# Layer two's rows scaled and split in 768-column operations, weights prepared at 0.64 steps, one branch hinted

## The chip, the cores and the metric

One core of a Trainium2 chip runs the whole program. The metric is the device time of one execution in microseconds (us). The engines are TensorE (PE in the rows; PEld is its weight load), VectorE (DVE), ScalarE (ACT), GpSimd (POOL) and SyncE (SP, which here only issues transfers). TensorE's clock has two levels, 1.2 and 2.4 GHz; the rows give the granted share of the higher one.

## The reference

Three stages in a row, all in fp32, on 7168 tokens of 192 columns.

```python
# 1. dynamic convolution: 8 heads of 24 columns, 7 taps, weights by softmax
out[b, s, h] = sum_k softmax(weight_gen)[b, s, h, k] * x_pad[b, s + k, h]
# 2. mixture of experts 1: 8 experts, two per token
noisy = x @ w_gate + log1p(exp(x @ w_noise)) * noise
top2, top2_w = two largest of noisy, softmax over the two
out[t] = sum over the two e:  top2_w * (relu(x[t] @ w1[e]) @ w2[e])     # w1 192x1024, w2 1024x192
# 3. mixture of experts 2: 8 experts, one per token
logits = normalised(x) @ normalised(expert_emb).T / tau
e = argmax(logits);  gate = softmax(logits)[e]
out[t] = gate * (relu(x[t] @ w1[e]) @ w2[e])
```

## The kernel before

**Layout.** Token columns: the 7168 tokens are 56 columns of 128. Work on tokens goes in chunks of four columns (`CH`), that is tiles of 128 partitions x 4 x 192 = 768 elements. Each layer handles its tokens in three groups of columns, 0 to 24, 24 to 40 and 40 to 56. Once a group is scored, its tokens are ranked by expert on the chip and listed into tiles of 256 tokens of one expert. GpSimd gathers a tile's rows from a DRAM table `T` (L1031), and scatters its results into `YB` (layer one, two rows per token) or the output (layer two) (L1115).

**Precision.** A row is scaled by a power of two (`pow2`, L254 to L256) and split into a high and a low fp16 part; products are made of three or five fp16 products that sum in PSUM. Weights are scaled and split in the same way: `prep_gen` reads fp32 weights, squares and sums them, scales them (L357, ScalarE), subtracts (L359, VectorE) and stores the fp16 parts to a DRAM table `WS`, from which SyncE loads a tile's weights (L1049).

**The tile loop.** Layer one has 64 tiles, 0 to 63, layer two 36, 64 to 99. Tiles 51 to 54 and the last four are rarely needed; they lie in a branch (`rare`, L1337), entered on a flag. Each iteration interleaves the first product of the next tile (`first_product`, L1081, ReLU copy L1083, its low part L1084) with the second product of this one (`second_product`, L1107). After a group of products each calls `bgq.point(share)`.

**Background queue.** Everything else is emitted by generators. A point adds its share (0.845) to two credits, one for VectorE (the real part) and one for ScalarE (the imaginary part); a generator goes on while both are above zero, and each `yield` takes what the step is said to cost. A `yield "lag"` ends a generator's turn at this point. There are eight points in an iteration with a full tile. A third thread holds `prep_rest`, layer two's weight preparation: it ignores the credits and makes `P_STEPS` steps per point once both attention groups 0 and 1 are emitted. `combine_gen(g)` loads the two result rows of a chunk from `YB` (`combine_load`, four buffers, two per chunk), scales one by its gate (L1162) and adds the other (L1169); it may start once the loop has reached tile 55 for groups 0 and 1, or 64 for group 2, and only when layer two's weights are `ready`. `post_chunk` then takes norms (L452), scales and splits the chunk, transposes it on TensorE (L492) and makes the scores (L506, L509). `ctl` picks experts (`choose2`, whose first operation is L529), ranks them and lists the tiles; its end allows a group's first gather. Two iterations ahead of a group's first gather, `bgq.finish` emits whatever is left of that group.

**What sets the order.** The program is planned before it runs: on each engine, within the stretch between two branches, the planner takes what it holds to be ready, by priority, which is the place of emission. Layer two's preparation has a low priority of its own (`R_LOW`), except for its loads, stores and small products, which take the place where they are emitted (`urgent`). Products of the background queue are held behind the tile product that was last emitted (`after_product`). Across the branch nothing moves.

**The branch.** `tc.If(flag > 0, preferred_fallthrough_block=False)` asks for the code of the side that is not entered right behind the comparison. Every engine loads the flag into a register and compares; the side not entered also settles the semaphores that the skipped block would have raised (L1337 in the rows).

Of the kernel before, what the change touches and what calls it, by code (L numbers as in the profile page):

```python
# [7 lines left out]
F32 = mybir.dt.float32  # L8
# [15 lines left out]
CH = 4  # L24
# [3 lines left out]
R_CTL, R_ATT, R_PREP, R_B, R_BODY = 0, 2000, 2000, 18000, 20000  # L28
C_AT = 5
R_LOW = 40000  # L30
P_STEPS = 0.54
SHARE = 0.845
ORDER = (0, 0, 1, 0, 1, 0, 1, 1)
LA = 3
# [44 lines left out]
def two_moe(ctx: ExitStack, tc: tile.TileContext, x, wgen, w_gate, w_noise, noise, w1a, w2a, emb, tau, w1b, w2b, out):  # L79
# [361 lines left out]
    isx = consts.tile([128, 2, NCOL], F32, name="isx")  # L441
    y_loads = []

    def post_chunk(l, acc, a, lg, g0, rows_i, done):
        ne = 16 if l == 0 else 8
        s = slice(a, a + CH)
        if rows_i is None:
# [5 lines left out]
        yield 1.6j  # L453
        pow2(nrm[:, l, s].bitcast(I32), sx[:, l, s], isx[:, l, s], CH, 194, 60)
        yield 0.4
        if l == 0:
            xs = att.tile([128, CH, D], F32, name="xs", bufs=1)
            for c in range(CH):
                A.activation(xs[:, c], acc[c], AF.Copy, scale=sx[:, l, a + c:a + c + 1])
            yield 1.4j  # L460
            A.activation(rows[:, :, 0:192], xs, AF.Copy)
            yield 0.7j
            for o, h, n in ((256, 0, 128), (192, 128, 64)):
                V.tensor_tensor(rows[:, :, o:o + n], xs[:, :, h:h + n], rows[:, :, h:h + n], op=ALU.subtract)
            V.tensor_copy(rows_i[:, :, 192:196].bitcast(F32), isx[:, 0, s, None].to_broadcast([128, CH, 4]))
            state["accs"] -= 1
            yield 1.0
        else:
            for c in range(CH):
                A.activation(rows[:, c, 0:192], acc[c], AF.Copy, scale=sx[:, l, a + c:a + c + 1])  # L470
            yield 1.4j
            for c in range(CH):
                for o, h, n in ((256, 0, 128), (192, 128, 64)):
                    V.scalar_tensor_tensor(rows[:, c, o:o + n], acc[c][:, h:h + n], sx[:, l, a + c:a + c + 1], rows[:, c, h:h + n],  # L474
                                           op0=ALU.mult, op1=ALU.subtract)
            state["accs"] -= 1
            yield 1.3
        if l == 0:
            write_rows(0, rows_i, a, CH)
        yield from lag(3)  # L480
# [670 lines left out]
    def combine_gen(g):  # L1151
        a, b = L2.groups[g]
        while 1 not in ready:
            yield None
        nxt = combine_load(a)
        yield from lag(5)
        for c0 in range(a, b, CH):
            y = nxt
            if c0 + CH < b:
                nxt = combine_load(c0 + CH)  # L1160
            for c in range(CH):
                V.tensor_scalar(y[0][:, c], y[0][:, c], gates[:, 0, c0 + c:c0 + c + 1], None, op0=ALU.mult)  # L1162
            yield 0.6
            while state["accs"] >= 2:
                yield None
            state["accs"] += 1
            acc = att.tile([128, CH, D], F32, name="acc")
            for c in range(CH):
                V.scalar_tensor_tensor(acc[:, c], y[1][:, c], gates[:, 1, c0 + c:c0 + c + 1], y[0][:, c], op0=ALU.mult, op1=ALU.add)  # L1169
            yield 1.1  # L1170
            bgq.chain(post_chunk(1, [acc[:, c] for c in range(CH)], c0, lgs[1][g], a, rows2[g][:, c0 - a:c0 - a + CH], dones[1][g]))

    def att_gen(g):
        a, b = L1.groups[g]
# [158 lines left out]
    def rare(block):  # L1333

        l, L = tiles[block[0]][0:2]
        c = L.np + KEEP
        with tc.If(nc.values_load(flag_i[l][0:1, c:c + 1], min_val=0, max_val=1) > 0, preferred_fallthrough_block=False):  # L1337
            new_block()
            state["rare"] = True
            for i in block:  # L1340
# [23 lines left out]
    for j, i in enumerate(seq):  # L1364
        later = seq[j + 1:j + 4]
        if len(later) >= LA:
            if later[LA - 1] in need:
                bgq.finish(need[later[LA - 1]])
            gather(later[LA - 1])
        one = first_product(later[0], bgq.point) if later else iter(())  # L1370
        two = second_product(i, bgq.point)
        for part in ORDER:
# [47 lines left out]
```

## Time and profile before

| | |
|---|---|
| time, median of three runs (lowest, highest) | 1059.68 us (1053.8, 1062.92) |
| time of the profiled execution | 1060.5 us |
| its span, first to last instruction | 1058.7 us |
| mean granted TensorE clock | 0.931 |
| TensorE products busy | 917.6 us, 87% of the span |
| TensorE weight loads busy | 826.0 us, 78% |
| VectorE busy | 691.1 us, 65% |
| ScalarE busy | 584.3 us, 55% |
| GpSimd busy | 380.9 us, 36% |
| DMA, over the span | 236.32 MB moved, mean 223 GB/s |

The profile is one execution on the chip. "Busy" is the time in which an engine had an instruction running; register work, branches, semaphores and the issue of transfers do not count as busy. A group of instructions is named by its line in the kernel, its engine and operation, and `out<-in` by the program's names; a bracket or a last field such as `5.89 <-issue` is the time that the engine stood idle ahead of it and what ended that; `issue` means that the profile shows nothing it waited for. `xh` as an output of L452, L470 and L474 is layer two's table of split rows, which lies in the same memory as the input.

### The profile page before, as it was taken

To read this page: it belongs to the slowest core of one execution; us is meant where nothing else is said; L and a number is where in the kernel's file an instruction comes from. 1 tells how busy PE (TensorE), PEld (TensorE's weight loads), DVE (VectorE), ACT (ScalarE), POOL (GpSimd) and SP (SyncE) were. 2 spreads that over 40 slices of the span, in tenths; PEclk is the share of its full clock that TensorE was granted. 3 is DMA by queue.
4 is the path that set the end of the run, shared out by engine and by line. 5 is a ranking of instruction groups with operands and counts; after the bars stand their busy time and mean duration, and the time that the engine had idled before them with its cause. 6 is when DMAs were issued, how large, how long until landed. Compare 5 with 4: busy or idle time off the path is not lost.

```text
span 1058.7 us, 26447 instructions
## 1 busy us (share of the span) xinstructions
PE 917.6 (87%) x9714; PEld 826.0 (78%) x9714; DVE 691.1 (65%) x1935; ACT 584.3 (55%) x1289; POOL 380.9 (36%) x368
## 2 busy tenths in 40 slices
PE   5993149998989999999998998995698999999996
PEld 2551139887979989989998987884587899999996
DVE  8996969898969879735353436679866753333331
ACT  2989426665548685445464546587156444444442
POOL 1000044434343653344444342321444344444522
PEclk9995559999989999999999998997698999999999
DMA  8789773745387756557989876852874734867661
GB/s 273 213 269 286 246 264 102 222 167 184 125 256 246 227 166 235 198 187 247 341 315 365 296 248 202 280 162 89 269 237 174 281 113 161 289 219 275 240 214 45
DMA packets 96392, 236.32 MB, mean 223 GB/s; under 512 B 13439, under 2 KB 64223, under 8 KB 87808
## 3 DMA queue, kind: packets, MB, share of 16 engines
q1 hardware_dynamic: 79360, 200.35, 55.3%
q0 software_dynamic: 16896, 34.20, 10.6%
q8 instruction: 80, 1.31, 0.5%
q14 instruction: 56, 0.46, 0.1%
HBM read 230.60 MB, written 57.90 MB: 273 GB/s over the span
## 4 chain that ended last, share of the span: by engine, by line
PE 53%; DVE 18%; DMA 11%; ACT 7%; issue 7%; POOL 2%; SPq 2%; POOLq 0%; DVEq 0%; ACTq 0%
PE ph L1081 24%; PE py L1107 21%; DMA xg<-t,gx 3%; DMA wb<-ws 3%; DVE tmp L407 2%; PE pt L1059 2%; DVE hl L1084 2%; DMA tmp<-yb 2%; PE py L434 2%; DVE acc L422 2%; ACT wo L357 1%; DVE wt L1084 1%; DVE acc L1169 1%; DVE xh L474 1%; DMA xh<-in_moe_w_dram 1%
## 5 line engine op out<-in xcount | busy, mean ns | idle before, releaser
L1081 PE MATMUL ph<-xt,wb 128*128 128x256 f16 x3360 | 429.1, 280 | 21.0 <-DMA wb<-ws 7.6
L1081 PEld LDWEIGHTS <-wb 128*128 128x128 f16 x3360 | 332.2, 100 | 64.2 <-issue 17.1
L1107 PE MATMUL py<-wb,hh 128*128 128x192 f16 x2688 | 357.5, 247 | 3.8 <-issue 3.8
L1083 ACT ACTIVATE hh<-ph 128x512 f16<-128x512 f32 (+1 forms) x368 | 210.0, 577 | 261.2 <-PE ph L1081 202.7
L1031 POOL DMA_INDIRECT xg<-t,gx x176 | 177.9, 1011 | 340.9 <-DVE gx L837 135.6
L1107 PEld LDWEIGHTS <-hh 128*128 128x128 f16 x2816 | 254.0, 98 | 9.7 <-issue 5.7
L1115 POOL DMA_INDIRECT yb<-ys,sx x116 | 126.3, 1089 | 202.6 <-ACT ys L1112 178.4
L1084 DVE SCALAR_TENSOR_TENSOR hl<-ph,hh 128x512 f16<-128x512 f32 (+1 forms) x184 | 117.3, 641 | 116.0 <-ACT hh L1083 83.1
L1084 DVE SCALAR_TENSOR_TENSOR wt<-ph,hh 128x512 f16<-128x512 f32 x184 | 125.6, 686 | 99.5 <-ACT hh L1083 78.1
L1107 PE MATMUL py<-wb,wt 128*128 128x192 f16 x736 | 182.0, 247 | 0.0
L1107 PE MATMUL py<-wb,hl 128*128 128x192 f16 x608 | 150.2, 247 | 0.0
L1112 ACT ACTIVATE ys<-py,sc 128x192 f32<-128x192 f32 x176 | 64.7, 416 | 89.8 <-PE py L1107 73.4
L1115 POOL DMA_INDIRECT out_dram<-ys,sx x60 | 61.8, 1029 | 102.0 <-ACT ys L1112 88.5
L407 DVE TENSOR_TENSOR tmp<-xh,wt 128x768 f32<-128x768 f32 x90 | 84.5, 949 | 0.3 <-PE ph L434 0.2
L1061 ACT ACTIVATE xt<-pt 128x768 f16<-128x768 f16 x84 | 67.7, 807 | 11.6 <-PE pt L1059 6.0
L1107 PEld LDWEIGHTS <-wt 128*128 128x128 f16 x736 | 72.5, 98 | 0.9 <-issue 0.7
L1092 DVE TENSOR_SCALAR sc<-xg,csl 128x2 f32<-128x2 f32 (+1 forms) x92 | 21.0, 228 | 75.4 <-ACT ys L1112 64.9
L1107 PEld LDWEIGHTS <-hl 128*128 128x128 f16 x672 | 66.0, 98 | 0.2
L1059 PE MATMUL pt<-identh,xg 128*128 128x128 f16 x528 | 47.0, 222 | 18.9 <-DMA xg<-t,gx 14.7
L1059 PEld LDWEIGHTS <-xg 128*128 128x128 f16 x528 | 36.9, 99 | 21.9 <-DMA xg<-t,gx 17.6
L359 DVE SCALAR_TENSOR_TENSOR wo<-xh,wsc,wo 128x384 f16<-128x384 f32 (+1 forms) x70 | 44.8, 667 | 2.8 <-ACT wo L357 1.9
L498 ACT ACTIVATE xt<-rb 128x768 f16<-128x768 f16 x56 | 42.7, 808 | 6.7 <-PE rb L492 6.5
(304 smaller groups left out, 992.7 us busy)
## 6 DMA issues: line engine op xcount, KB each, us to landing
wb<-ws SPq DMA_DIRECT2D x84, 1024.0 KB
wb<-ws SPq DMA_DIRECT2D x84, 768.0 KB
ws<-wo SPq DMA_DIRECT2D x16, 768.0 KB
tmp<-yb SPq DMA_DIRECT2D x28, 384.0 KB
ws<-wo SPq DMA_DIRECT2D x16, 512.0 KB
ws<-wo SPq DMA_DIRECT2D x32, 256.0 KB
xh<-ws SPq DMA_DIRECT2D x8, 1024.0 KB
xh<-in_moe_w_dram SPq DMA_DIRECT2D x10, 768.0 KB
```

Of the source, the lines that this page charges most:

```text
L359: V.scalar_tensor_tensor(lo, v, sc[:, c:c + 1], h, op0=ALU.mult, op1=ALU.subtract)
L407: V.tensor_mul(dst.rearrange("p t (h g) -> p (t h) g", g=G), xv, w)
L498: A.activation(xt.rearrange("p a n -> p (a n)"), pa[:, 0:768], AF.Copy)
L1031: PL.indirect_dma_start(out=xg[:, h], out_offset=None, in_=T[l][0:rows_in], in_offset=bass.IndirectOffsetOnAxis(ap=gidx[l][:, u + h:u + h ...
L1059: PE.transpose(pt[:, j, h], xg[:, h, 128 * b:128 * b + 128], identh)
L1061: A.activation(xt.rearrange("p j h n -> p (j h n)"), pt.rearrange("p j h n -> p (j h n)"), AF.Copy)
L1081: state["pe"] = mark = PE.matmul(ph[:, q, :n], s, m, start=j == 0, stop=j == 4)
L1083: A.activation(hh[:, fs, :n], ph[:, :, :n], AF.Relu)
L1084: state["pin"] = V.scalar_tensor_tensor(hl[:, fs, :n], ph[:, :, :n], 0.0, hh[:, fs, :n], op0=ALU.max, op1=ALU.subtract)
L1107: state["pe"] = PE.matmul(py[:, h], t[:, f, hs], w2[:, f, c], start=f == 0 and j == 0, stop=f == 7 and j == 2)
L1112: A.activation(ys[:, h], py[:, h], AF.Copy, scale=sc[:, h:h + 1])
L1115: d = PL.indirect_dma_start(out=dst, out_offset=bass.IndirectOffsetOnAxis(ap=sidx[l][:, u + h:u + h + 1], axis=0), in_=ys[:, h], in_offset ...
```

## The change

Four edits.

- `P_STEPS`, the steps of layer two's weight preparation per point, goes from 0.54 to 0.64.
- The gate scaling in `combine_gen`, four VectorE operations of 192 columns, becomes one of 768 columns with the gate broadcast. The credits asked go from 0.6 and 1.1 to 0.9 and 1.6.
- `post_chunk` for layer two scales the chunk with one VectorE operation of 768 columns into a single fp32 buffer `xs`, converts it with one ScalarE copy of 768 columns, and subtracts with two VectorE operations of 512 and 256 columns. Before, ScalarE made four scaled copies and VectorE eight scale-and-subtract operations. The credits asked go from 1.4j and 1.3 to 0.9, 0.7j and 1.1. Layer one's operations stay, but it asks 1.1 in place of 1.0 at the end. The chunk's buffer is counted as free once it is scaled.
- The branch gets a label and no preferred side, and ahead of the products of the iteration that ends at layer one's rare block a hint "LikelyTaken" for that label is given to TensorE, behind the last product emitted. Layer two's branch, behind the last tile, gets no hint.

```diff
@@ -28,7 +28,7 @@
 R_CTL, R_ATT, R_PREP, R_B, R_BODY = 0, 2000, 2000, 18000, 20000
 C_AT = 5
 R_LOW = 40000
-P_STEPS = 0.54
+P_STEPS = 0.64
 SHARE = 0.845
 ORDER = (0, 0, 1, 0, 1, 0, 1, 1)
 LA = 3
@@ -441,7 +441,7 @@
     isx = consts.tile([128, 2, NCOL], F32, name="isx")
     y_loads = []
 
-    def post_chunk(l, acc, a, lg, g0, rows_i, done):
+    def post_chunk(l, acc, a, lg, g0, rows_i, done, whole=None):
         ne = 16 if l == 0 else 8
         s = slice(a, a + CH)
         if rows_i is None:
@@ -453,28 +453,22 @@
         yield 1.6j
         pow2(nrm[:, l, s].bitcast(I32), sx[:, l, s], isx[:, l, s], CH, 194, 60)
         yield 0.4
+        xs = att.tile([128, CH, D], F32, name="xs", bufs=1)
         if l == 0:
-            xs = att.tile([128, CH, D], F32, name="xs", bufs=1)
             for c in range(CH):
                 A.activation(xs[:, c], acc[c], AF.Copy, scale=sx[:, l, a + c:a + c + 1])
             yield 1.4j
-            A.activation(rows[:, :, 0:192], xs, AF.Copy)
-            yield 0.7j
-            for o, h, n in ((256, 0, 128), (192, 128, 64)):
-                V.tensor_tensor(rows[:, :, o:o + n], xs[:, :, h:h + n], rows[:, :, h:h + n], op=ALU.subtract)
+        else:
+            V.tensor_tensor(xs, whole, sx[:, l, s, None].to_broadcast([128, CH, D]), op=ALU.mult)
+            yield 0.9
+        state["accs"] -= 1
+        A.activation(rows[:, :, 0:192], xs, AF.Copy)
+        yield 0.7j
+        for o, h, n in ((256, 0, 128), (192, 128, 64)):
+            V.tensor_tensor(rows[:, :, o:o + n], xs[:, :, h:h + n], rows[:, :, h:h + n], op=ALU.subtract)
+        if l == 0:
             V.tensor_copy(rows_i[:, :, 192:196].bitcast(F32), isx[:, 0, s, None].to_broadcast([128, CH, 4]))
-            state["accs"] -= 1
-            yield 1.0
-        else:
-            for c in range(CH):
-                A.activation(rows[:, c, 0:192], acc[c], AF.Copy, scale=sx[:, l, a + c:a + c + 1])
-            yield 1.4j
-            for c in range(CH):
-                for o, h, n in ((256, 0, 128), (192, 128, 64)):
-                    V.scalar_tensor_tensor(rows[:, c, o:o + n], acc[c][:, h:h + n], sx[:, l, a + c:a + c + 1], rows[:, c, h:h + n],
-                                           op0=ALU.mult, op1=ALU.subtract)
-            state["accs"] -= 1
-            yield 1.3
+        yield 1.1
         if l == 0:
             write_rows(0, rows_i, a, CH)
         yield from lag(3)
@@ -1158,17 +1152,16 @@
             y = nxt
             if c0 + CH < b:
                 nxt = combine_load(c0 + CH)
-            for c in range(CH):
-                V.tensor_scalar(y[0][:, c], y[0][:, c], gates[:, 0, c0 + c:c0 + c + 1], None, op0=ALU.mult)
-            yield 0.6
+            V.tensor_tensor(y[0], y[0], gates[:, 0, c0:c0 + CH, None].to_broadcast([128, CH, D]), op=ALU.mult)
+            yield 0.9
             while state["accs"] >= 2:
                 yield None
             state["accs"] += 1
             acc = att.tile([128, CH, D], F32, name="acc")
             for c in range(CH):
                 V.scalar_tensor_tensor(acc[:, c], y[1][:, c], gates[:, 1, c0 + c:c0 + c + 1], y[0][:, c], op0=ALU.mult, op1=ALU.add)
-            yield 1.1
-            bgq.chain(post_chunk(1, [acc[:, c] for c in range(CH)], c0, lgs[1][g], a, rows2[g][:, c0 - a:c0 - a + CH], dones[1][g]))
+            yield 1.6
+            bgq.chain(post_chunk(1, [acc[:, c] for c in range(CH)], c0, lgs[1][g], a, rows2[g][:, c0 - a:c0 - a + CH], dones[1][g], acc))
 
     def att_gen(g):
         a, b = L1.groups[g]
@@ -1334,7 +1327,7 @@
 
         l, L = tiles[block[0]][0:2]
         c = L.np + KEEP
-        with tc.If(nc.values_load(flag_i[l][0:1, c:c + 1], min_val=0, max_val=1) > 0, preferred_fallthrough_block=False):
+        with tc.If(nc.values_load(flag_i[l][0:1, c:c + 1], min_val=0, max_val=1) > 0, label=f"rare{l}"):
             new_block()
             state["rare"] = True
             for i in block:
@@ -1367,6 +1360,10 @@
             if later[LA - 1] in need:
                 bgq.finish(need[later[LA - 1]])
             gather(later[LA - 1])
+        if later and later[0] > i + 1:
+
+            with after_product():
+                tc.mark_branch_hint_location(f"rare{tiles[i][0]}", "LikelyTaken", [mybir.EngineType.PE])
         one = first_product(later[0], bgq.point) if later else iter(())
         two = second_product(i, bgq.point)
         for part in ORDER:
```

## Rows read from the trace of the kernel before

**Rows 1.** The page: busy tenths and granted TensorE clock in 40 equal slices of the span.

```profile
PE   5993149998989999999998998995698999999996
...
PEclk9995559999989999999999998997698999999999
```

**Rows 2.** The chain that ended last: start us, length us, what.

```profile
475.08 1.98 PE py L1107 x24
...
483.75 1.98 PE py L1107 x24
...
642.69 4.19 DMA tmp<-yb
...
679.80 8.16 DMA tmp<-yb
...
759.77 4.42 PE ph L1081 x20
```

**Rows 3.** Windows: length, each engine's busy us (instructions), granted clock, DMA share, GB/s.

```profile
633.00:642.50 9.50, 3.93 (x22) 2.83 (x23) 0.92 (x2) 1.05 (x3) 2.02 (x2) 0.64 0.56 205
642.50:672.00 29.50, 27.26 (x290) 25.04 (x288) 26.30 (x90) 22.92 (x66) 11.30 (x11) 1.00 0.73 236
672.00:695.00 23.00, 23.00 (x256) 21.87 (x254) 12.63 (x35) 12.57 (x30) 5.35 (x6) 1.00 0.82 281
695.00:759.00 64.00, 42.45 (x543) 35.06 (x542) 54.94 (x281) 39.27 (x110) 19.86 (x14) 0.78 0.48 151
759.00:1059.00 300.00, 280.13 (x3104) 262.17 (x3103) 135.24 (x397) 131.78 (x279) 119.56 (x117) 0.97 0.60 206
230.00:430.00 200.00, 188.60 (x2079) 176.00 (x2077) 172.64 (x487) 126.80 (x269) 87.64 (x80) 0.97 0.62 204
```

**Rows 4.** One line each, windows behind 632 us: duration min/median/max ns, first and last start.

```profile
L492 PE MATMUL rb<-identh,xh x168: 216/219/314, 695.4 to 820.6; 128*128 128x128 f16 x168
...
L529 DVE TENSOR_REDUCE mx<-lg x3: 277/286/334, 724.2 to 826.6; 128x16 f32<-128x128 f32 x2, 128x24 f32<-128x192 f32 x1
...
L1031 POOL DMA_INDIRECT xg<-t,gx x16: 952/957/1002, 751.4 to 788.2; - x16
...
L359 DVE SCALAR_TENSOR_TENSOR wo<-xh,wsc,wo x8: 599/604/607, 648.1 to 670.9; 128x384 f16<-128x384 f32 x8
```

**Rows 5.** The branch's line: duration min/median/max ns, first and last start us.

```profile
L1337 PEldq COMPARE_BRANCH  x4: 81/1954/5529, 631.7 to 1049.9; - x4
...
L1337 POOLq INC_SWDGE_SEM  x2: 852/1542/2231, 640.3 to 1054.0; - x2
```

**Rows 6.** Timeline of TensorE from 632 to 650 us: start, length, products, idle before.

```profile
638.57 4.04 PE L1081 MATMUL ph<-xt,wb 128*128 128x256 f16 x20 [5.89 <-issue]
...
648.96 1.26 PE L1081 MATMUL ph<-xt,wb 128*128 128x256 f16 x10
```

**Rows 7.** Timeline of VectorE around chunks of layer two: start, length, operations, idle before.

```profile
646.91 1.23 DVE L1162 TENSOR_SCALAR tmp<-tmp,gates 128x192 f32<-128x192 f32 x4 [2.89 <-DMA tmp<-yb]
...
785.44 1.00 DVE L1162 TENSOR_SCALAR tmp<-tmp,gates 128x192 f32<-128x192 f32 x4
...
791.93 1.92 DVE L474 SCALAR_TENSOR_TENSOR xh<-acc,sx,xh 128x128 f16<-128x128 f32 x8
```

**Rows 8.** All groups by line and shape: busy us, mean ns of one.

```profile
L1083 ACT ACTIVATE hh<-ph 128x512 f16<-128x512 f32 x336 | 197.7, 595 | 243.1 <-PE ph L1081 201.3 <-issue 14.1 <-PE pt L1059 9.3
...
L407 DVE TENSOR_TENSOR tmp<-xh,wt 128x768 f32<-128x768 f32 x90 | 84.5, 949 | 0.3 <-PE ph L434 0.2
...
L470 ACT ACTIVATE xh<-acc,sx 128x192 f16<-128x192 f32 x56 | 21.0, 446 | 5.3 <-DVE isx L256 3.7 <-DVE wo L359 1.6
...
L461 ACT ACTIVATE rows<-xs 128x768 f16<-128x768 f32 x14 | 11.8, 846 | 0.0
...
L464 DVE TENSOR_TENSOR rows<-xs,rows 128x512 f16<-128x512 f32 x14 | 9.6, 685 | 1.6 <-ACT rows L461 1.6
...
L464 DVE TENSOR_TENSOR rows<-xs,rows 128x256 f16<-128x256 f32 x14 | 5.8, 417 | 0.0
```

## The prediction

> **What bounds the kernel now.** I read the 40-slice page first: TensorE is at 9 tenths nearly everywhere, with three dents: the head (before about 150 us), a dent near 635 us, and a wide one from about 695 to 765 us, where the granted clock falls too [rows 1]. Outside the dents TensorE sets the pace: tile after tile starts 8.67 us apart [rows 2] (475.08 to 483.75). So I read the stretch behind 633 us alone, in windows [rows 3]: from 642.5 to 695 us TensorE is busy 50.3 of 52.5 us; from 695 to 759 us it is busy 42.5 of 64 us, part of that at half clock, while VectorE is busy 54.9 of 64 us. After 759 us TensorE is busy 280 of 300 us and VectorE 135, so the rest of layer two is a TensorE stretch again. The hole is the wait for layer two's first routing: TensorE's last tiles of layer one run out before group 0 of layer two is combined, scored and listed.
>
> Next, why that is late. Group 0's loads of YB start at 642.69 us, but the fourth chunk's only at 679.80 us [rows 2]; the first score transpose of layer two runs at 695.4 us, the first choice of an expert at 724.2 us, the first gather at 751.4 us [rows 4], the first product at 759.77 us [rows 2]. That is not transfer time: one pair of loads landed in 4.19 to 8.16 us. It is the order in which the code is emitted. I stepped through the queue by its yields: a point makes P_STEPS steps of the weight preparation, a tile has 8 points. Preparation of layer two starts in tile 7 and needs 205 steps; 205/0.54 = 380 points, so it ends in tile 59, and the generator that combines waits for that. Group 0 is then emitted in tiles 60 and 61, most of it in the forced finish ahead of tile 61, and the transposes are pinned behind the product of that moment. The last eight splits of prepared weights, 648.1 to 670.9 us, agree [rows 4].
>
> **The branch.** TensorE's queue holds four compare-and-branches; the longest took 5529 ns and the shortest 81 [rows 5], and before the products at 638.57 us TensorE stood 5.89 us with nothing to wait for [rows 6]. Behind that pause 20 products took 4.04 us, where later 10 take 1.26; the granted clock from 633 to 642.5 us averages 0.64, so part of it ran at the lower level, 1.2 GHz, and 1.5 us were lost [rows 3, 6]. The change drops the layout preference and hints the branch to TensorE. If the target is then there in time, the branch costs like the short ones: TensorE gains 5.4 + 1.5 = 6.9 us. If not, 0. Below nothing: a hint that fetches the wrong side could add another jump of up to 5.5 us. I take 6.9, at three in four. What the row shows is one long jump and one short one. The Trainium skill (Runtime: NRT & Kernel Launch, section Instruction fetch mechanics) says that a taken branch whose target is outside the fetch window stalls on a fetch; the trace agrees with the 5.53 us. By it the skip stays a far jump and the gain would be 0, which is a rival below.
>
> The 6.9 us are not all on the path. SyncE and GpSimd cross the same branch on their own: the GpSimd step that ends it took up to 2231 ns [rows 5], and the first YB load goes out only at 642.69 us. TensorE back earlier ends layer one's tiles earlier, and without the rest of the change it would mostly widen the hole. What is late next: group 0's routing.
>
> **Preparation at 0.64.** 205/0.64 = 320 points, so it ends in tile 48, before the branch. Three effects. (a) Group 0 may be emitted from tile 55 on. (b) Eight splits and their scalings leave the stretch after 642.5 us: 8 x 604 ns = 4.8 us of VectorE there [rows 4], as much on ScalarE. (c) The work is denser before: 56 splits, about 34 us, over 320 instead of 380 points; at 8.67 us a tile that is 10 instead of 8 per cent of VectorE. From 230 to 430 us VectorE is busy 172.6 of 200 us and TensorE idle 11.4 [rows 3], so the price is 0 to 3 us; I take 1, since the splits have the lowest priority. Their loads come 16% denser on SyncE's queue; DMA is at 0.62 there [rows 3], which covers them.
>
> **Wide operations.** Per chunk of four columns (14 chunks) VectorE loses four gate scalings, 1.23 us as a group, and eight subtractions, 1.92 us [rows 7]; it gains two operations on 128x768, 949 ns each by the nearest row (a broadcast multiply of the same shape), and two subtractions of 685 and 417 ns [rows 8]: 3.15 out, 3.00 in. ScalarE loses four scaled copies (21.0/14 = 1.50 us) and gains one of 0.85 us [rows 8]. So VectorE is about even: 14 x -0.15 = -2 us, or +1 by the tighter group of scalings, 1.00 us [rows 7]; I take 0. ScalarE's 9 us are hidden behind TensorE outside the hole.
>
> Here a rule speaks against the change. The rows give a merged multiply no loss, because four small operations cost four starts. The Trainium skill (VectorE: DVE Perf Modes, section Mode 2×_2P — use both read ports for one tensor) says that an fp32 tensor_scalar gets two elements a cycle and a tensor_tensor one. By it the merge would add, as an estimate from that page, 0.4 us per chunk or 5.6 us in all. The measured group of four disagrees.
>
> The pacing changes as well. A chunk now asks 4.9 us of VectorE credit where it asked 3.4, with 0.6 for its scores 5.5; at 0.845 a point that is 6.5 points. Six chunks and five lags are 44 points; tiles 55 to 60 have 48. So group 0 fits in just ahead of tile 61, spread under products that TensorE has anyway. Its loads then stand on SyncE's queue among the weight loads of those tiles, and one that waits for a free buffer holds the weight load behind it, and TensorE after that. VectorE once stood 2.89 us for such a load [rows 7]; six of them bound this at 0 to 17 us. I take 2, since a pair that lands in 4 to 8 us has a tile and more to land in.
>
> **The sum.** Tile 61 starts at about 695 us now (the first transposes, pinned there). With 6.9 us from the branch and the 2 us of waits: 690. Last scores 4 us later, 694. From the first choice to the first gather 751.4 - 724.2 = 27.2 us: 721. Gather to product 8.4 us: 729.6. That is 30 us before 759.77. The other bound is VectorE: from 642.5 to 759 us it did 93.9 us [rows 3], less 5 for the splits 89; at the 89% of the window from 642.5 to 672 us this takes 100 us, so the start would be 742.5, 17 us earlier, with nothing left over. Started at 729.6, about 12 us of group 1's work is left to lie beside the first five tiles of layer two, and costs 0 to 12. Between 17 and 30 I take 23, nearer to neither, and 1 off for the denser preparation: 22. The profiled execution took 1060.5 us (span 1058.7 and 1.8 around it), 0.8 above the median of 1059.68. 1060.5 - 22 = **1038 us**. This case by itself: 1060.5 - 30 - 6 (half clock avoided in the hole) = 1024 to 1060.5 - 17 + 6 = 1050.
>
> **Rivals.** *The hint does nothing*: 5.89 us stay, most of it inside the hole's shift; about 5 us less gain, 1043. For it: the skip must still jump. It lies in the forecast's range.
> *The hole stays*: the four YB buffers, two chunks' worth, hold up the loads and not the order; then only the 0 to 7 us of the branch are left, and 1053 to 1060. For it: VectorE is 89% busy right after 642.5 us. Against: it is busy only 12.6 of 23 us from 672 to 695 [rows 3], when no chunk was loaded.
> *Slower*: the new relay. Each chunk goes VectorE, ScalarE, VectorE through the single xs buffer where four columns were pipelined before. VectorE's queue is in order; if nothing is placed between, it stands through the copy (0.85) and one hidden-layer copy ahead of it on ScalarE (0.6) [rows 8], 1.4 us a chunk, 14 x 1.4 = 20 us, in the very stretch where VectorE sets the end. If the hole also stays, 1060 - 7 + 20 = 1073. It decides once the standing exceeds 22/14 = 1.6 us per chunk against the full gain, or 0.5 against the branch alone. Against: hidden-layer splits and the next chunk's work can fill it.
>
> **Chances.** Forecast 0.63 (a quarter of it without the hint), hole stays 0.21, slower 0.16. Less or more than 1% is the bound of what runs of this kernel can tell from no change: faster 0.65, same 0.20, slower 0.15. The range 1022 to 1065 takes in the forecast's bounds and the staying hole.
>
> **What would show it.** TensorE's branch near 630 us under 0.5 us and no half clock behind it; the first transposes of layer two before 670 us instead of 695.4; the first choice near 695, the first gather near 721, the first product near 730; no splits of weights after the branch; VectorE without pauses waiting for ScalarE's copy of xs. If the first product stays near 755 the order was not what held group 0; if it moves and the end does not, group 1 or 2 gives the time back as a wait ahead of tiles 69 or 77.

## The result, and the profile after

The changed kernel took 1047.12 us (median of four runs, 1045.22 to 1047.76) where the kernel before took 1058.06 beside it: a ratio of 0.9892, 95% interval [0.9845, 0.9939]. A second measurement gave 0.9877 [0.9854, 0.9901]. That is 11 us (13 between the two profiled executions), half of the forecast 22. The time lies inside the range of 1022 to 1065, which is wide enough to take in the staying hole as well. The profiled execution took 1047.76 us, span 1045.7, mean granted clock 0.940 (0.931 before).

The page's busy tenths of TensorE and its granted clock in 40 slices, to be laid beside [rows 1]:

```profile
PE   5993149999989999989999997987799998999996
...
PEclk9995559999989999998999999998899998999998
```

The hole between 695 and 765 us is shallower, and there is a small new dent, 8 in both lines, in the seventh slice from the end (863 to 889 us). The windows (length, each engine's busy us, granted clock, DMA share, GB/s) answer to [rows 3]:

```profile
642.50:672.00 29.50, 24.05 (x260) 22.04 (x258) 20.62 (x51) 16.95 (x52) 10.55 (x9) 0.94 0.71 228
672.00:695.00 23.00, 20.67 (x267) 19.46 (x266) 18.05 (x52) 16.27 (x41) 10.33 (x7) 1.00 0.80 271
695.00:759.00 64.00, 51.28 (x634) 45.76 (x632) 50.66 (x207) 34.88 (x81) 23.18 (x19) 0.87 0.56 172
...
855.00:885.00 30.00, 25.85 (x244) 22.29 (x242) 9.34 (x24) 8.50 (x17) 12.69 (x13) 0.89 0.36 111
```

From 695 to 759 us TensorE is busy 51.3 us instead of 42.5: the hole gave back almost 9 us. From 855 to 885 us it is busy 25.9 of 30, at clock 0.89, with VectorE, ScalarE and GpSimd each busy for less than half of it: that is new.

The steps, one line each, behind 560 us (duration min/median/max ns, first and last start us), as in [rows 4]:

```profile
L486 PE MATMUL rb<-identh,xh x168: 216/219/311, 664.0 to 822.9; 128*128 128x128 f16 x168
...
L523 DVE TENSOR_REDUCE mx<-lg x3: 286/286/348, 711.7 to 827.5; 128x16 f32<-128x128 f32 x2, 128x24 f32<-128x192 f32 x1
...
L1025 POOL DMA_INDIRECT xg<-t,gx x20: 942/955/1927, 733.4 to 799.0; - x20
...
L359 DVE SCALAR_TENSOR_TENSOR wo<-xh,wsc,wo x8: 611/618/623, 582.4 to 586.6; 128x384 f16<-128x384 f32 x8
```

The splits of weights end at 586.6 us instead of 670.9, the first transposes of layer two stand at 664.0 instead of 695.4, the first choice at 711.7 instead of 724.2, the first gather at 733.4 instead of 751.4.

The branch's line, then TensorE's timeline (start, length, products, idle before), as in [rows 5, 6]:

```profile
L1330 PEldq COMPARE_BRANCH  x2: 393/1946/3499, 635.8 to 1034.7; - x2
...
L1330 POOLq INC_SWDGE_SEM  x2: 852/1542/2231, 644.5 to 1041.1; - x2
```

```profile
638.68 2.34 PE L1075 MATMUL ph<-xt,wb 128*128 128x256 f16 x20 [1.83 <-DVEq L1330]
...
652.89 1.85 PE L1075 MATMUL ph<-xt,wb 128*128 128x256 f16 x10 [4.30 <-DVE hl L1078]
```

The hinted branch of layer one took TensorE 0.393 us instead of 5.529; the unhinted one behind the last tile took 3.499, and 3.810 in the kernel before, so that it is the hint and not the lost layout preference that shortens it. The pause fell from 5.89 to 1.83 us (what is left ends with VectorE's own crossing), and 20 products behind it took 2.34 us instead of 4.04. But 14 us later TensorE stands 4.30 us for the hidden layer's low part. VectorE's timeline shows why:

```profile
641.74 0.69 DVE L1078 SCALAR_TENSOR_TENSOR hl<-ph,hh 128x512 f16<-128x512 f32 x1 [0.40 <-ACT hh L1077]
650.23 0.96 DVE L1155 TENSOR_TENSOR tmp<-tmp,gates 128x768 f32<-128x768 f32 x1 [7.79 <-DMA tmp<-yb]
```

VectorE stood 7.79 us for the first load of YB, with the next low part queued behind it. The planned order puts that load right behind the branch.

And the new dent, on TensorE and then on GpSimd:

```profile
867.13 0.24 PE L1101 MATMUL py<-wb,hh 128*128 128x192 f16 x1 [0.22 <-issue]
867.86 0.24 PE L1101 MATMUL py<-wb,hh 128*128 128x192 f16 x1 [0.49 <-issue]
...
869.29 0.32 PE L1101 MATMUL py<-wb,hh 128*128 128x192 f16 x2 [1.10 <-issue]
...
870.73 0.24 PE L1101 MATMUL py<-wb,hl 128*128 128x192 f16 x1 [0.87 <-issue]
...
872.14 0.32 PE L1101 MATMUL py<-wb,hl 128*128 128x192 f16 x1 [1.01 <-issue]
872.85 0.50 PE L1101 MATMUL py<-wb,hh 128*128 128x192 f16 x2 [0.39 <-issue]
...
873.58 4.44 PE L1075 MATMUL ph<-xt,wb 128*128 128x256 f16 x20
```

```profile
860.61 0.99 POOL L1025 DMA_INDIRECT xg<-t,gx  x1 [7.93 <-PE ph L1075]
861.91 1.00 POOL L1109 DMA_INDIRECT out_dram<-ys,sx  x1 [0.30 <-issue]
...
869.58 0.95 POOL L1025 DMA_INDIRECT xg<-t,gx  x1 [0.30 <-issue]
870.83 0.95 POOL L1025 DMA_INDIRECT xg<-t,gx  x1 [0.30 <-issue]
```

Nothing that the profile shows was waited for; a few products ran between the pauses, 4.1 us of pauses in all, and the 20 products behind them took 4.44 us, where 20 took 2.34 above: the lower clock. From 860.61 to 871.8 us GpSimd issued nine indirect transfers in a row, 0.3 us apart; the pauses begin 6.3 us into that run.

Where each stretch is gained is seen from the starts of tiles' first products, against the profile of before (us; tile 64 is layer two's first). The experiments are in it too; those marked * were run where the kernel before took 1036.5 us, 20 less than elsewhere, and no profile of it was taken there, so only their course from tile to tile counts.

| profile | 31 | 47 | 56 | 64 | 69 | 74 | 77 | 95 |
|---|---|---|---|---|---|---|---|---|
| before, start | 459.6 | 593.4 | 638.6 | 759.8 | 822.7 | 872.5 | 898.5 | 1037.3 |
| after | +0.6 | +4.2 | +0.1 | -9.2 | -21.2 | -23.1 | -13.8 | -13.8 |
| preparation alone | +0.9 | -1.7 | -1.5 | -11.4 | -23.4 | -22.6 | -20.3 | -20.3 |
| hint alone | +2.9 | -0.7 | -4.8 | -3.3 | -3.6 | -4.0 | -4.0 | -4.0 |
| wide alone | -7.9 | -10.1 | -9.7 | -12.9 | -20.4 | -21.9 | -14.5 | -14.5 |
| after, spaced | -2.2 | -3.5 | -7.6 | -24.6 | -31.3 | -32.3 | -31.1 | -27.0 |
| preparation, spaced more | -1.3 | -6.0 | -5.7 | -20.4 | -35.1 | -28.9 | -28.4 | -28.4 |
| no preparation* | -16.0 | -21.9 | -22.0 | -30.9 | -47.1 | -46.3 | -45.1 | -45.1 |
| no hint* | -6.8 | -12.5 | -12.5 | -32.8 | -50.3 | -52.1 | -51.0 | -51.0 |
| no wide* | -8.1 | -13.7 | -17.8 | -35.6 | -52.3 | -51.8 | -51.8 | -51.8 |
| after, burst* | -6.3 | -11.9 | -16.0 | -33.0 | -50.4 | -52.3 | -51.1 | -51.1 |

The changed kernel stands 23.1 us ahead at tile 74, about the forecast 22, and loses 9.3 of it by tile 77.

### The profile page after: what moved, and what is told of

Its sections match the earlier page's. It is cut to its first block, busy times and chain, and to the rows that moved or that the text cites. A ratio compares the mean times of both kernels' runs of the same rounds, so it can differ in the third digit from the quotient of the medians.

```text
span 1045.7 us, 26257 instructions
## 1 busy us (share of the span) xinstructions
PE 912.2 (87%) x9714; PEld 821.5 (79%) x9714; DVE 689.8 (66%) x1823; ACT 577.4 (55%) x1247; POOL 393.2 (38%) x368
## 4 chain that ended last, share of the span: by engine, by line
PE 51%; DVE 22%; DMA 7%; ACT 7%; issue 7%; SPq 2%; POOL 2%; another core or an unknown queue 0%; POOLq 0%; DVEq 0%; ACTq 0%
PE ph L1075 23%; PE py L1101 21%; DVE tmp L407 3%; DVE hl L1078 2%; DVE acc L422 2%; DVE wt L1078 2%; DMA xg<-t,gx 2%; PE py L434 2%; PE pt L1053 2%; DMA xh<-in_moe_w_dram 2%; ACT wo L357 2%; DVE wo L359 1%; ACT junk L311 1%; DMA wb<-ws 1%; ACT xt L492 1%
## 5 line engine op out<-in xcount | busy, mean ns | idle before, releaser
L1075 PE MATMUL ph<-xt,wb 128*128 128x256 f16 x3360 | 422.5, 277 | 27.1 <-DVE hl L1078 11.3
L1075 PEld LDWEIGHTS <-wb 128*128 128x128 f16 x3360 | 328.3, 99 | 71.1 <-issue 30.5
L1025 POOL DMA_INDIRECT xg<-t,gx x176 | 186.2, 1058 | 323.7 <-DVE gx L831 135.5
L1101 PEld LDWEIGHTS <-hh 128*128 128x128 f16 x2816 | 255.4, 99 | 14.5 <-issue 10.5
L1109 POOL DMA_INDIRECT yb<-ys,sx x116 | 130.4, 1124 | 201.1 <-ACT ys L1106 179.3
L1101 PE MATMUL py<-wb,hl 128*128 128x192 f16 x608 | 152.4, 251 | 3.6 <-issue 3.6
L1053 PE MATMUL pt<-identh,xg 128*128 128x128 f16 x528 | 45.7, 220 | 12.7 <-DMA xg<-t,gx 10.7
L422 DVE TENSOR_TENSOR acc<-acc,tmp 128x768 f32<-128x768 f32 x48 | 45.7, 953 | 0.5
```

Of the source, the lines that this page charges most:

```text
L422: V.tensor_add(acc, acc, tmp)
L1025: PL.indirect_dma_start(out=xg[:, h], out_offset=None, in_=T[l][0:rows_in], in_offset=bass.IndirectOffsetOnAxis(ap=gidx[l][:, u + h:u + h ...
L1053: PE.transpose(pt[:, j, h], xg[:, h, 128 * b:128 * b + 128], identh)
L1075: state["pe"] = mark = PE.matmul(ph[:, q, :n], s, m, start=j == 0, stop=j == 4)
L1101: state["pe"] = PE.matmul(py[:, h], t[:, f, hs], w2[:, f, c], start=f == 0 and j == 0, stop=f == 7 and j == 2)
L1109: d = PL.indirect_dma_start(out=dst, out_offset=bass.IndirectOffsetOnAxis(ap=sidx[l][:, u + h:u + h + 1], axis=0), in_=ys[:, h], in_offset ...
```

## The experiments

My theory after the result: the parts did what they were to do as far as tile 74, and back-to-back indirect transfers on GpSimd then make TensorE pause. The rivals: a part works against the others; or the pauses belong to that place of the program.

**Each part alone.** Preparation (`e1`):

```diff
-P_STEPS = 0.54
+P_STEPS = 0.64
```

> The kernel before with weights prepared at 0.64 steps alone. Order theory (group 0 of layer two is late because it is emitted late): the first score transposes of layer two come before 675 us instead of 695.4, layer two's first product comes 5 to 15 us earlier, and the time falls by 6 to 14 us. Work theory (VectorE's amount of work sets the stretch): only the 5 us of weight work that leave the stretch are gained, 2 to 6 us. In both, TensorE still stands about 5.9 us at the branch.

Measured: 1040.51 us, ratio 0.9856 [0.983, 0.9881]. First transposes 657.2 us, first product of layer two 748.4, and 2.3 us given back from tile 74 to 77. That is the order theory, with 15 us where it said 6 to 14. This part alone is at least as fast as all three.

The hint (`e2`):

```diff
-with tc.If(..., preferred_fallthrough_block=False):
+with tc.If(..., label=f"rare{l}"):
...
+tc.mark_branch_hint_location(f"rare{tiles[i][0]}", "LikelyTaken", [mybir.EngineType.PE])
```

> The kernel before with the labelled and hinted branch alone. Order theory: TensorE's 5.89 us at the branch become about 1.8, no lower clock behind it, but layer two's first product is still held by group 0's routing, so it comes 0 to 4 us earlier and the time falls by 0 to 4 us. Branch theory (the branch carries the whole gain): the time falls by 8 us or more.

Measured: 1058.26 us, ratio 1.0021 [0.9992, 1.005]: nothing. TensorE's timeline of it:

```profile
633.82 2.34 PE L1081 MATMUL ph<-xt,wb 128*128 128x256 f16 x20 [1.83 <-DVEq L1337]
...
648.20 1.88 PE L1081 MATMUL ph<-xt,wb 128*128 128x256 f16 x10 [4.44 <-DVE hl L1084]
```

The pause at the branch is 4 us shorter and the wait for YB takes 4.4, as in the changed kernel. So that wait is the hint's other side, not that of the wide operations: the load leaves hardly earlier, at 641.76 us instead of 642.69, in both kernels 0.2 us after the GpSimd step that ends the branch.

The wide operations (`e3`): the edits of `post_chunk` and `combine_gen` in the change, and nothing else.

> The kernel before with the wide operations alone (with their credits). Order theory: the first transposes stay near 695 us, the time moves by -3 to +4 us. Work theory: VectorE has 1 to 3 us less work between the branch and layer two's first product, and the time falls by 2 to 6 us. Relay theory (VectorE stands for ScalarE's copy of xs): slower by 4 us or more, with waits of the subtractions for that copy above 0.5 us a chunk.

Measured: 1046.74 us, ratio 0.9913 [0.9896, 0.9929], where the sum had called them even. 10.1 us are there at tile 47 already. VectorE's last eight splits stand at 623.9 to 627.6 us, inside the branch's pause, instead of 648.1 to 670.9 [rows 4]:

```profile
L359 DVE SCALAR_TENSOR_TENSOR wo<-xh,wsc,wo x8: 611/612/619, 623.9 to 627.6; 128x384 f16<-128x384 f32 x8
```

Stepping through the queue, these splits are emitted in the iterations of tiles 55 to 58, hardly earlier than before (55 to 59). But the small product that they need, which is pinned behind the tile product last emitted, now falls into the iteration ahead of the branch; before, it ran at 642.45 us, behind the branch:

```profile
622.38 0.17 PE L330 MATMUL rb<-wnr,sel 128*128 128x4 bf16 x1
```

So the planner could place the splits ahead of the branch, and work does move across it, against "Across the branch nothing moves". In the queue the credit of 1.1 in place of 1.0 is enough to shift this product (it adds two points to layer one's finish), and the counter that is lowered sooner does not; on the chip neither was run alone. This part, too, loses 7.4 us from tile 74 to 77, with the same kind of pauses behind a run of eight transfers.

**Spacing the gathers** (`e4`): the changed kernel with one small GpSimd operation ahead of each gather of the two tiles behind a group's first.

```diff
+                if any(f < i < f + 3 for f in firsts):
+                    with tc.issue_after(state["gather"].ins):
+                        gap = PL.tensor_tensor(work.tile([128, 4], F32, name="gap", bufs=1), half[:, 0:4], half[:, 0:4], op=ALU.pow)
+                    order.enter_context(tc.issue_after(gap.ins))
```

> The changed kernel with a small power operation on GpSimd (4 columns, about 0.9 us) ahead of each gather of the second and third tile of a group, so that gathers that wait for a listing don't leave back to back. Burst theory (TensorE's pauses with nothing to wait for come from runs of eight and more transfers that GpSimd issues back to back): the pauses near 464, 782 and 868 us go, the 9 us lost between tiles 74 and 77 shrink below 4, and the time falls by 6 to 15 us against the changed kernel. Fetch theory (the pauses are late instruction loads of TensorE, whatever GpSimd does): the pauses stay where they are, the time is that of the changed kernel within 3 us.

Measured: 1034.74 us, ratio 0.9802 [0.9781, 0.9823], though GpSimd does more. From tile 74 to 77 it loses 1.2 us instead of 9.3, but 4.1 more by tile 78, behind a run of eight gathers and scatters that were not spaced. The loss of the changed kernel from tile 31 to 32, 8.2 us behind another run of eight, shrinks to 2.5, one tile later. So the burst theory hit the time, about 10 us, but not the pauses: they are still there near 473, 743, 783 and 873 us, each behind a run of six to eight transfers that this spacing left. And only 4 us of the 13 between the two kernels at tile 95 arise behind tile 74; 7.7 are there at tile 47. The added operations change the plan as well, so this run alone doesn't show the pauses to be the cause.

**One part taken out, and a burst added.** Without the preparation (`e5`: 0.64 back to 0.54), without the hint (`e6`: the branch's old line back), without the wide operations (`e7`), and the changed kernel with eight gathers more (`e8`):

```diff
+        if i == 88:
+            for k in range(8):
...
+                with tc.issue_after(last.ins):
+                    last = PL.indirect_dma_start(out=e, out_offset=None, in_=T[l][0:rows_in],
+                                      in_offset=bass.IndirectOffsetOnAxis(ap=gidx[l][:, u:u + 1], axis=0))
```

> The changed kernel with the preparation back at 0.54 steps (hint and wide operations stay). If the gain of the wide operations (1046.7 alone) comes from the plan and the hint is worth nothing on the path: 1046, within 3, first product of layer two near 745 us. If the hint's 4 us at the branch reach the end once something behind it has moved: 1042 to 1043. If the preparation is what carries the changed kernel's gain: back to 1054 to 1058.

> The changed kernel without the hint, with the old layout preference (0.64 and wide operations stay). If the hint is worth nothing: 1047, within 2. If the parts add up (15 us of the preparation and 9 of the wide operations, each alone): 1031 to 1034, so that the hint would cost the changed kernel its difference. If the hint's 4 us reach the end: 1051.

> The changed kernel with the old operations on small columns (0.64 and the hint stay). If the hint is worth nothing: as the preparation alone, 1040.5, within 2.5. If the hint's stall behind the branch (VectorE standing for the first YB load, 4 us) costs the path what it gave: 1040 to 1045. If the hint's 4 us reach the end: 1036. If the changed kernel's give-back at tiles 74 to 77 comes from the hint's shift and not from the wide operations: 1047.

> The changed kernel with eight more indirect loads, issued back to back behind those of tile 88, into spare buffers that nothing reads, in a stretch (about 920 to 940 us) where TensorE is gap-free now. If runs of back-to-back indirect transfers on GpSimd make TensorE's sequencer pause: pauses of 0.3 to 1.2 us without a releaser, 3 to 8 us in all, begin 5 to 8 us into the run, with a fall of the clock behind them; 1050 to 1057 in all. If the pauses at tiles 74 to 77 have another cause (code loading at that place, or the moment of the schedule): no pause there, and 1047 to 1049.

These four ran together where the kernel before took 1036.53 us; the expectations in us have to be read as ratios to 1056. Measured: 0.9805 [0.9774, 0.9835] without the preparation, 0.9752 [0.9722, 0.9783] without the hint, 0.9743 [0.9712, 0.9774] without the wide operations, 0.9762 [0.9732, 0.9793] with the burst. Every one gained more than the changed kernel elsewhere. The changed kernel without the burst was not run there, so the burst's price rests on its profile. Two windows of it, of the added run (20 transfers in a row) and of group 2's first gathers (15):

```profile
899.00:926.00 27.00, 27.00 (x318) 25.89 (x316) 9.30 (x17) 12.14 (x24) 19.55 (x20) 1.00 0.86 293
...
836.00:866.00 30.00, 30.00 (x327) 28.42 (x326) 9.96 (x17) 12.80 (x24) 17.35 (x19) 1.00 0.76 255
```

TensorE never stood, and none of the four profiles gives back more than 2.1 us between tiles 69 and 95. From 230 to 1030 us they show not one pause above 0.2 us without a releaser, but for the unhinted branch; the profiles of the other sets show 6 to 24 us of them. So my expectation of the burst failed here. Either the pauses have another cause, or they need a condition that this set did not have.

**The changed kernel and the burst on one chip again** (`e9`, unaltered; `e10`, the edit of `e8`):

> The changed kernel itself, unaltered, beside the burst below. The chips differ: the kernel before took 1056 to 1058 us where TensorE's pauses under runs of indirect transfers were seen, and 1036.5 where none of four profiles showed any. If the pauses are what took half of the forecast gain: a ratio of 0.987 to 0.991 on a chip that shows them at tiles 74 to 77, and 0.973 to 0.977 on one that does not (as its three parts, taken out one at a time, gave there). If something else in the changed kernel took it: 0.987 to 0.991 on either.

> The changed kernel with eight more indirect loads back to back behind those of tile 88, as before, now beside the changed kernel on the same chip. On a chip that shows pauses at tiles 74 to 77, if runs of indirect transfers make them: 3 to 8 us of pauses without a releaser begin 5 to 8 us into the added run, and 4 to 12 us more than the changed kernel; if the pauses belong to that place of the program: none there, and 0 to 2 us more. On a chip without pauses: none, and 0 to 2 us more.

Measured, beside a kernel before of 1059.18 us: 1047.93 us, 0.9877 [0.9854, 0.9901], for the changed kernel; 1057.85 us, 0.999 [0.9975, 1.0005], with the burst. Eight loads that nothing reads cost 9.9 us. The windows of the same tiles, first of the changed kernel, then with the burst:

```profile
938.00:954.00 16.00, 16.00 (x197) 15.44 (x195) 5.45 (x11) 6.14 (x14) 7.01 (x8) 1.00 0.82 312
```

```profile
936.00:952.00 16.00, 9.57 (x96) 7.74 (x95) 1.98 (x4) 2.69 (x6) 10.65 (x11) 0.83 0.86 298
952.00:960.00 8.00, 8.00 (x69) 7.42 (x69) 1.47 (x5) 3.01 (x7) 2.84 (x3) 0.70 0.23 71
```

GpSimd's and TensorE's timelines with the burst:

```profile
936.76 0.99 POOL L1025 DMA_INDIRECT xg<-t,gx  x1 [1.61 <-PE pt L1060]
938.06 0.98 POOL L1032 DMA_INDIRECT tmp<-t,gx  x1 [0.31 <-issue]
...
946.88 0.95 POOL L1032 DMA_INDIRECT tmp<-t,gx  x1 [0.30 <-issue]
```

```profile
942.52 0.38 PE L1082 MATMUL ph<-xt,xh 128*128 128x128 f16 x4 [1.13 <-issue]
943.95 0.22 PE L1082 MATMUL ph<-xt,xh 128*128 128x128 f16 x1 [1.05 <-issue]
...
945.38 0.33 PE L1108 MATMUL py<-wb,hh 128*128 128x192 f16 x2 [0.97 <-issue]
...
946.81 0.48 PE L1108 MATMUL py<-wb,hh 128*128 128x192 f16 x2 [1.02 <-issue]
...
948.92 0.48 PE L1108 MATMUL py<-wb,hh 128*128 128x192 f16 x2 [1.48 <-issue]
```

A gap-free stretch turned into one with the same signature: the first pause 4.6 us into the run, then one after another until 3 us behind its end, and the clock down behind them (0.70). So the added run of indirect transfers makes the pauses; the place in the program does not. Nor does the amount of traffic: the gap-free window of the changed kernel has a DMA share of 0.82 and 312 GB/s, the one with the pauses 0.86 and 298. And it does so in one set and not in another.

**A better version.** The preparation at 0.64 with the spacing, without hint and wide operations (`e11`), and with the spacing on five tiles behind each first instead of two (`e12`: `f + 6` for `f + 3`).

> The kernel before with the preparation at 0.64 and the spacing of the gathers as in the spaced run, without hint and wide operations. Where the pauses show: the preparation alone gave back only 2 us behind its peak of 23.4, so with the spacing 1033 to 1038 (ratio 0.978 to 0.982), the same as the changed kernel with the spacing, if hint and wide operations are worth nothing then; 1028 to 1031 if wide operations and hint were a cost under it, 1039 to 1042 if the spacing only mends what they bring. On a chip without pauses: 0.974 to 0.977.

> The same with the spacing on the gathers of five tiles behind each first instead of two. If runs of transfers that are left (six to eight, with the scatters, from the third tile on) still cost pauses: 3 to 5 us less than the run beside it, with no pauses left behind 750 us. If GpSimd's added work, about 1.3 us for each gather, delays the gathers of those tiles into TensorE's path: 0 to 8 us more. On a chip without pauses: equal or up to 3 us more.

Measured: 1035.67 us, 0.9797 [0.9753, 0.984], and 1030.62 us, 0.9744 [0.97, 0.9788], beside a kernel before of 1056.69. The second is the fastest beside a kernel before of this speed. In its window of group 2's first gathers TensorE is gap-free at full clock, where the changed kernel has 25.9 of 30 (the preparation alone has 28.4, and with the first spacing 29.9):

```profile
850.00:880.00 30.00, 30.00 (x327) 28.43 (x326) 10.51 (x18) 13.92 (x26) 23.92 (x24) 1.00 0.59 188
```

What the wider spacing adds, 5 us in the end, arises mostly at group 0's first gathers: against the other it is 2 us ahead at tile 64 and 8 at tile 65. There seven transfers in a row are left with the first spacing, and no such run with the second. The windows, first of the first spacing:

```profile
738.00:758.00 20.00, 16.05 (x163) 14.12 (x163) 12.55 (x71) 6.84 (x14) 8.95 (x10) 0.91 0.82 251
```

```profile
738.00:758.00 20.00, 19.39 (x212) 18.04 (x211) 19.12 (x84) 7.89 (x16) 14.00 (x14) 1.00 0.95 310
```

The expectation of no pauses behind 750 us failed: five are left, 2.6 us in all. The ratio of this second kernel is that of three kernels of the set without pauses (0.9743 to 0.9762), its time isn't: 1030.6 us against 1010 to 1012. By the record both sets ran on the chip of the same number, 13, so the pauses do not go with a chip alone. The hint and the wide operations add nothing to the preparation that these runs can tell: under the spacing 0.9797 without them and 0.9802 with them, and in the other set the preparation with the one, the other or both gave 0.9743 to 0.9762.

## Why the prediction came out as it did

**The branch, 6.9 us priced.** TensorE's jump fell to 0.393 us, and the lower clock behind it is gone: right. The size was 5.8 us: 1.7 for the clock (1.5 priced) and 4.1 for the pause (5.4 priced), because TensorE now waits for VectorE's crossing. "One long jump and one short one" misreads the row: besides layer one's 5.529 us it holds 3.810 us for layer two's branch. "Mostly not on the path" was right, too: alone it is worth nothing. By the Trainium skill (Runtime: NRT & Kernel Launch, section Instruction fetch mechanics) a taken branch whose target is outside the fetch window stalls on a fetch; the unhinted 3.499 us agree, and the hinted 0.393 us show a skip of the same kind without that stall.

**The waits for YB, 2 us priced, bound 0 to 17.** One wait, 7.79 us of VectorE and 4.30 of TensorE. It is not behind a weight load but at the first load behind the branch, and the hint alone brings it (2.89 us of VectorE before). But the term left out more than waits. From tile 57 to 62 TensorE takes 61.5 us instead of 47.1. Of these 14.4 us, 6.6 are idle, the 4.30 among them, and 7.7 are products: group 0's transposes and scores, which used to run in the hole, now run here. "Spread under products that TensorE has anyway" left out that TensorE has this work to do itself.

**The preparation.** The order was right: the splits end before the branch and group 0 is emitted from tile 55. (Its loads come 19% denser, not 16: 0.64 against 0.54.) The price of the denser preparation, 1 us, is open: alone it shows no loss by tile 47 (-1.7), with the wide operations the changed kernel stands 10 us behind the one without it at tile 47 in the set without pauses (-11.9 against -21.9). One way to it is that the preparation does not wait for the credits but is charged to them, so that a denser one slows the rest of the queue; that this makes the 10 us is not shown. There, taking it out costs 4.2 us at the end (1016.37 against 1012.18 with the burst), so it is not additive with the wide operations.

**The wide operations, 0 priced.** VectorE's work is even as forecast, as the groups show against [rows 8] (busy us, mean ns):

```profile
L1155 DVE TENSOR_TENSOR tmp<-tmp,gates 128x768 f32<-128x768 f32 x14 | 13.3, 952 | 8.2 <-DMA tmp<-yb 8.2
L462 DVE TENSOR_TENSOR xs<-acc,sx 128x768 f32<-128x768 f32 x14 | 13.3, 949 | 0.0
...
L468 DVE TENSOR_TENSOR xh<-xs,xh 128x512 f16<-128x512 f32 x14 | 9.6, 689 | 2.2 <-ACT hh L1077 1.3 <-ACT xh L465 0.5
```

VectorE's total went from 691.1 to 689.8 us. The relay that was to make it slower cost 2.2 us of waits in 14 chunks, not 20. The part still gains 9 us alone, as far as is seen by the plan: the splits in the branch's pause, and 10 us in layer one, whose work it does not touch except for one credit (1.0 to 1.1) and a counter that is lowered sooner. Which of these moved layer one was not tried. By the Trainium skill (VectorE: DVE Perf Modes, section Mode 2×_2P — use both read ports for one tensor) an fp32 tensor_scalar gets twice the rate of a tensor_tensor, by which the merge would lengthen the scaling; the measured 0.952 us against 1.00 to 1.23 for the four [rows 7] shows no loss.

What the pricing missed is what the larger credits do to group 2: by the queue its choice is emitted in the iteration of tile 70, with the preparation alone in that of 69. The last write of group 2's list, in the changed kernel and with the preparation alone:

```profile
L837 DVE TENSOR_SCALAR gx<-dfv x3: 167/177/184, 732.5 to 859.6; 128x10 int32<-128x10 f32 x1, 128x16 int32<-128x16 f32 x1, 128x38 int32<-128x38 f32 x1
```

```profile
L843 DVE TENSOR_SCALAR gx<-dfv x3: 165/174/183, 727.5 to 851.3; 128x10 int32<-128x10 f32 x1, 128x16 int32<-128x16 f32 x1, 128x38 int32<-128x38 f32 x1
```

TensorE starts tile 74 at 849 to 850 us in both. So the list comes 10 us behind it with the wide operations and 1.4 without.

**The hole: 44 points, and 30 us earlier.** This step failed in part. Group 0's chunks and scores were to be emitted in 44 points ahead of tile 61. Stepping through the queue of the changed kernel again, they take 52, of which 48 lie ahead of it; the forced finish then takes 35, the last scores, the choice and the list, with group 1's first chunks between. With the preparation alone the finish takes 22 points, as a chunk asks less credit. The larger miss is TensorE's: the iteration of tile 61, which starts with tile 62's first product, was to start at 690 us and started at 708.8, mostly for the 14.4 us above and the 4.2 by which layer one was late. So the first choice came at 711.7 us, not 694. From choice to gather it took 21.7 us (27.2 priced), from gather to product 17.2 (8.4 priced), in part because scores of group 1 stand in TensorE's order ahead of tile 64 and wait 4.8 us for ScalarE's copies; the longer of two waits:

```profile
743.02 0.70 PE L500 MATMUL rb<-rw,xt 128*128 128x8 f16 x9 [3.30 <-ACT xt L492]
```

The first product came 9.2 us earlier, not 17 to 30.

**The rest of layer two stays as it is.** Group 1 caught up behind tile 68 (12.7 us ahead there, 21.2 at tile 69), so that 23.1 us stood at tile 74, where the sum had 22. That this agrees is luck: the sum had all of it at tile 64. The step that failed decides the end: that what is won by then is kept. With TensorE 23 us earlier and group 2's list only 2 us earlier (859.6 for 861.7), the gathers of three tiles wait for the list and leave in one run, where before they left in pairs. The prediction looked for a wait ahead of tile 77; it was pauses between tiles 74 and 77 during and after the run. How much they cost goes with how late the list is: 9.3 us in the changed kernel and 7.4 with the wide operations alone, in runs of nine and eight, but 2.3 with the preparation alone, in a run of six, and nothing with the hint alone. So of the rivals, a part that works against the others is in it, too: where the pauses show, the wide operations lengthen the run. The late list by itself costs little: in the set without pauses the changed kernel with the burst had its list 10 us behind tile 74 as well and gave back 1.2. Another run of eight cost 8.2 us at tile 31. The kernel before had such pauses as well, at 301 to 307 us behind eight transfers, and I had read them as part of TensorE's idle 11.4 us from 230 to 430 [rows 3].

**What stays open.** What TensorE lacks in these pauses, why they are there in most sets and not in one, and why the kernel before was 20 us faster in that set: the pauses that its profile elsewhere shows from 230 us on, 9 us without the branch, are less than that. The runs show that a burst makes them and that they are few where all gathers are spaced, not the mechanism.

## What to carry to other kernels

When a critical stage moves earlier, look at what was held for it and will leave at once. Two changes that move the same stage forward are not a sum; time each alone and each left out, beside the whole on the same chip at the same time. An operation that costs no more can still come later: look at what its credits do to the order. Shortening a branch on one engine is worth no more than the engine that crosses it last allows.

## What was not expected of the hardware

- Where the kernel before took 1056 to 1059 us, behind eight or nine indirect transfers in a row on GpSimd, 1.25 to 1.3 us apart, TensorE stopped for 0.2 to 1.5 us at a time, from 5 to 6 us into the run, with a fall of the granted clock behind it: 9 to 11 us for each of the two long runs at 860 and 937 us. With about 1 us of other GpSimd work between the gathers such a stretch was gap-free (850 to 880 us). Where the kernel before took 1036.5 us, 15 and 20 in a row did nothing.
- With a hint TensorE's skip of layer one's branch took 0.38 to 0.48 us in every run, without it 5.53 to 5.99; layer two's, never hinted, took 3.45 to 4.14.
- The first load of YB left 0.2 to 0.5 us behind the end of a GpSimd step that settles semaphores at the branch and took 2.231 us, with the hint and without it; so a shorter jump of TensorE did not bring it forward.
